# The last stores issued with their evictions, the last product in halves, and the prologue's work shared out anew

## The chip, the cores and the metric

The kernel runs on one NeuronCore of one Trainium2 chip. The metric is the device time of one execution in microseconds (us); what is compared is the median of several runs. The engines are called by the profile's names: PE is TensorE (matmul), DVE is VectorE, ACT is ScalarE, POOL is GpSimd, SP is SyncE, which issues nearly all DMAs here.

## The reference

Attention inside chunks of 64 tokens, then a feed-forward layer with softplus in its middle:

```python
def _attn_ref(q, k, v):                      # each 8 x 8 x 576 x 64 (batch, head, token, head_dim)
    q_c = q.reshape(B, H, nc, chunk, D)      # chunk = 64, so nc = 9; k_c and v_c alike
    scores = scale * np.matmul(q_c, k_c.transpose(0, 1, 2, 4, 3))
    scores = scores - np.max(scores, axis=-1, keepdims=True)
    attn = np.exp(scores)
    attn = attn / (np.sum(attn, axis=-1, keepdims=True) + 1e-09)
    return np.matmul(attn, v_c).reshape(B, H, S, D)

def _moe_ref(x, w_in, w_out):                # x 4608 x 512, w_in 512 x 2048, w_out 2048 x 512
    h = x @ w_in
    g = np.maximum(h, 0.0) + np.log1p(np.exp(-np.abs(h)))
    return g @ w_out
```

## The kernel before

**Tiling.** The 4608 tokens are 36 attention blocks of 128 tokens (two chunks, all eight heads), and nine row groups `m` of 512 tokens (four blocks, `TPM = 4` tiles each) for the two matrix products. The hidden width of 2048 is cut into 16 slices `fc` of 128. So there are 144 GEMM blocks `g = 16 m + fc`. Each has a first product `G1` (`gemm1`, L587: 12 matmuls of 128x512 into a PSUM tile `pa`), a softplus on ACT (`sp_g`, L595), a split of its result into a rounded part `g_hi` (`sp_hi`, L599, ACT) and a remainder `g_lo` (`sp_lo`, L603, DVE or POOL), and a second product `G2` (`gemm2`, L618: three terms for each of four tiles, added up in the PSUM tiles `po0` to `po3` over the 16 blocks of a row group). PE runs `G2` of a block behind `G1` of the next. In row group 0 both products run their three terms one after the other, `wi_lo` in the second term of `G1`, `x` low part in the third, `g_lo` in the third term of `G2`, so that late operands have more time.

**Split weights.** Each product is three f32r matmuls (high times high, high times low, low times high). The weights arrive as f32 in 32 units (`units`, numbered by when they are due; one for each `fc` of `w_in` and of `w_out`). Each unit is loaded (`w_load`, 512 KB) and decoded in five steps: `w_top` (L252, ACT or POOL), `w_low` (L261, ACT), `w_add` (L266, DVE, 128x1024), `w_hi` (L287, ACT or POOL) and `w_lo` (L291, DVE or POOL). `TOP_ACT`, `HI_POOL` and `LO_POOL` list the unit numbers that go to the engine in the list's name; `NORM_POOL` and `GLO_POOL` do the same for the division by the softmax sum (`att_norm`, L537, by attention block) and for `sp_lo` (by GEMM block).

**Attention.** The first four blocks (`FIRST_BLK = 4`) run on PE before the first GEMM block: transposes (`pe_t`), scores (`pe_s`), the subtraction of the row maximum as a matmul with a negated identity (`pe_sub`, L518, for blocks in `SUB_PE`; otherwise `att_sub`, L512, on DVE), exp on ACT, sum and reciprocal on DVE (`att_den`, L530), `att_norm`, a transpose (`pe_e`) and the product with V (`pe_v`, L403), whose result goes to `x` as a rounded part on ACT (`att_xh`, L562) and a remainder on DVE (`att_xl`, L566). All other blocks are transposed by DVE or DMA and run their PE work in pairs, as bursts (`blk_s` L462, `blk_v` L550) behind `G1` of GEMM blocks 4, 8, 15 and later ones. Their transposes on DVE are four small instructions (`blk_t4` L449 for `q` and `k`, `blk_e4` L486 for the weights after exp, for blocks in `SWAP_DVE`) or one (`blk_t` L439, `blk_e` L474).

**The order.** A list scheduler (`Plan`) simulates the engines with a written-in cost for each task, takes at each moment the ready task with the smallest `urg`, and emits the code in that order. The order so found is fixed: each engine runs its instructions in it and waits where an operand is late. `T0` and `TG` say when GEMM block `g` is due (`T0 + TG * g`), and the weights' and the bursts' urgencies follow from that; `VQ`, `KS`, `LQ` and `QK_URG` move other urgencies, `LOAD_AFTER`, `QK_AFTER` and `V_AFTER` name the load behind which the weight loads, the burst blocks' loads of `q` and `k`, and their loads of `v` may start.

**Filler matmuls.** Where the planner's own times leave PE a gap of more than 0.6 us before its time 90, `keep_warm` (L335) puts matmuls of the identity (`ident`) ahead of the task, whether or not the gap is there on the chip:

```python
    def keep_warm(dst):
        for _ in range(int(FILL * (plan.gap - 0.6) / 0.23)):     # FILL = 0.8
            nc.tensor.matmul(dst[:, :P], ident, ident, start=True, stop=True)
```

Such a matmul is f32 and stands in the trace as two records, in the order as one row.

**Halves.** With `HALVES = 2` GEMM blocks 0 and 1 each run as two pieces of two tiles (256 columns of `G1`), so that the first piece needs the attention of two blocks only.

**The end.** For the last row group, `evacuate` (L627) copies `po0` and `po2` on ACT and `po1` on DVE into `raw` tiles, tasks of their own (`store`, L632) send each 256 KB out over SP, and the fourth tile goes out as two halves (`last_half`: half a is copied and sent by ACT, half b copied by DVE and sent by SP, behind half a's copy).

Of the kernel before, what the change touches and what calls it, by code (L numbers as in the profile page):

```python
# [148 lines left out]
def chunked_attention_softplus_ffn(  # L149
# [9 lines left out]
    nc = tc.nc  # L159
    B, H, S, D = q.shape  # L160
    DM, DF = w_in.shape
    P = 128
# [444 lines left out]
    def gemm2(w):  # L607
        if w["first"]:
            pos.setdefault(w["m"], []).extend(po_tile(t) for t in w["tiles"])
        g_hi, g_lo, fc = w["hi"], w["lo"], w["fc"]  # L610
        w_hi_, w_lo_ = wo[fc]
        if w["first"]:
            keep_warm(pos[w["m"]][w["tiles"][0]])
        terms = ((g_hi, w_hi_), (g_hi, w_lo_), (g_lo, w_hi_))
        tiles = list(enumerate(w["tiles"]))
        order = [(n, j) for n in range(3) for j in tiles] if w["m"] < 1 else [(n, j) for j in tiles for n in range(3)]
        for n, (j, t) in order:
            nc.tensor.matmul(  # L618
                pos[w["m"]][t], terms[n][0][:, j * P : (j + 1) * P], terms[n][1],
                start=(w["first"] and n == 0), stop=(w["last"] and n == 2),  # L620
            )

    def evacuate(w, t):
        if t % 2 == 0:
            live["out", w["m"], t // 2] = raw_tile()
        o = live["out", w["m"], t // 2][:, t % 2 * DM : (t % 2 + 1) * DM].bitcast(F32)
        (nc.vector.tensor_copy if t % 2 else nc.scalar.copy)(o, pos[w["m"]][t])  # L627
        live["o", w["m"], t] = o

    def store(m, t):  # L630
        r0 = m * MT + t * P
        nc.sync.dma_start(out[r0 : r0 + P, :], live.pop(("o", m, t)))  # L632

    def last_half(w, j):
        m, t = w["m"], TPM - 1
# [4 lines left out]


    plan = Plan(raw=RAW_BUFS, top=TOP_BUFS, low=LOW_BUFS, po0=1, po1=1, po2=1, po3=1, pa=2, g=LAG + 1, u=1)
    HALVES = 2
    SPLIT = 0
    SUB_PE = (0, 1, 2, 3)
    SP_FREE = 1
    OFF = 0
    NOFF = 3
    T0, TG = 30.0, 5.2
    TK = (0,1)  # L650
    KS = 0.2
    VQ = -40
    LQ = -61
    HI_POOL = (1,3,5,6,7,8,9,10,12,13,15,17,19,20,21,25,27,28,30,31)
    WHOLE = (4,5,9)
    SWAP_DVE = (4,7,9)
    LOAD_POOL = ()
    TOP_ACT = (0,1,3,4,5,6,7,8,9,10,15,16,17,18,19,20,23,24,25,27,29,30)
    LOAD_AFTER = "v3"
    LO_POOL = (1,2,4,5,7,8,9,14,15,16,19,22,23,25,26,27,28,29,31)  # L660
    NORM_POOL = (0,2,3,4,5,6,7)
    GLO_POOL = (0,2,4,5,6,8,9,10,12,15,16,17,19)
    WO_AFTER = 1.1
    BEGIN = (4, 8, 15)
    BURST_AT = (6, 14)
    QK_AFTER = "v3"
    V_AFTER = "load10"
    K6_AFTER = "load13"
    QK_URG = 0
    T_URG = 0  # L670
    V_URG = 20
    SW_URG = 0
# [170 lines left out]
    for w in ahead + blocks:  # L843
# [21 lines left out]
        if w["last"]:  # L865
            for t in range(TPM):
                odd = t % 2
                if m == NM - 1 and t == TPM - 1:
                    for j in range(2):
                        plan.add(f"ev{m}_{t}" + "ab"[j], "DVE" if j else "ACT", 0.4, partial(last_half, w, j), [f"G2_{g}"],  # L870
                                 urg=-3, after=[f"ev{m}_{t - 1}"])
                    continue
                plan.add(f"ev{m}_{t}", "DVE" if odd else "ACT", 0.65, partial(evacuate, w, t), [f"G2_{g}"], urg=-3,
                         take=[] if odd else [("raw", [f"st{m}_{j}" for j in (t, t + 1) if m < NM - 1 or j < TPM - 1])],
                         after=[f"ev{m}_{t - 1}"] if odd else [])
                plan.add(f"st{m}_{t}", "SP", 0.6, partial(store, m, t), [f"ev{m}_{t}"], urg=1e5, kb=256)

    plan.emit()

# [33 lines left out]
```

## Time and profile before

| what | value |
|---|---|
| median of 3 runs | 862.52 us (862.5 to 862.55) |
| the profiled execution | 862.54 us |
| its span in the profile | 860.7 us (so 1.84 us lie around the span) |
| PE busy in the span | 848.0 us (99%) |
| DVE, ACT, POOL busy | 344.5, 313.7, 75.1 us (40%, 36%, 9%) |
| bytes moved | 63.13 MB, mean 73 GB/s |
| TensorE clock granted | 0.999 of full speed |

A busy engine need not be working at its peak, and idle time of the other engines costs nothing as such. Start times below are from the start of the span; a row that stands for several instructions gives their time together.

### The profile page before, as it was taken

To read this page: it belongs to the slowest core of one execution; us is meant where nothing else is said; L and a number is where in the kernel's file an instruction comes from. 1 tells how busy PE (TensorE), PEld (TensorE's weight loads), DVE (VectorE), ACT (ScalarE), POOL (GpSimd) and SP (SyncE) were. 2 spreads that over 40 slices of the span, in tenths; PEclk is the share of its full clock that TensorE was granted. 3 is DMA by queue.
4 is the path that set the end of the run, shared out by engine and by line. 5 is a ranking of instruction groups with operands and counts; after the bars stand their busy time and mean duration, and the time that the engine had idled before them with its cause. 6 is when DMAs were issued, how large, how long until landed. Compare 5 with 4: busy or idle time off the path is not lost.

```text
span 860.7 us, 14812 instructions
## 1 busy us (share of the span) xinstructions
PE 848.0 (99%) x5886; PEld 701.4 (81%) x5886; DVE 344.5 (40%) x600; ACT 313.7 (36%) x493; POOL 75.1 (9%) x76
## 2 busy tenths in 40 slices
PE   8899999999999999999999999999999999999997
PEld 7688888888888888888888888888888888888886
DVE  4989865333433241515252433324332514121111
ACT  3857744322423242424242423224232424232222
POOL 1576751000000000000000000000000000000000
PEclk9999999999999999999999999999999999999999
DMA  9887833222231224222322223222412241010001
GB/s 228 231 215 189 217 94 94 47 46 51 42 98 40 51 43 101 42 57 35 86 56 59 39 53 96 43 50 44 99 40 53 42 102 40 11 50 0 1 1 49
DMA packets 207061, 63.13 MB, mean 73 GB/s; under 512 B 184592, under 2 KB 200464, under 8 KB 206992
## 3 DMA queue, kind: packets, MB, share of 16 engines
q1 hardware_dynamic: 206848, 62.06, 31.6%
q8 instruction: 46, 0.75, 0.4%
q14 instruction: 23, 0.19, 0.1%
q10 hardware_dynamic: 144, 0.13, 0.0%
HBM read 45.09 MB, written 9.44 MB: 63 GB/s over the span
## 4 chain that ended last, share of the span: by engine, by line
PE 91%; DVE 3%; SPq 1%; DMA 1%; ACT 1%; issue 1%; POOL 0%; DVEq 0%; POOLq 0%; ACTq 0%
PE po L618 44%; PE pa L587 43%; PE pa L550 2%; PE pa L462 2%; SPq L318 1%; DMA raw<-in_moe_w_in_dram 1%; DMA raw<-in_moe_w_out_dram 1%; DVE qe L449 1%; DVE eT L486 0%; DVE ka L449 0%; ACT u L595 0%; DVE den L530 0%; DVE low L266 0%; DVE wib L266 0%; DVE x L566 0%
## 5 line engine op out<-in xcount | busy, mean ns | idle before, releaser
L595 ACT ACTIVATE u<-pa 128x512 f32<-128x512 f32 (+1 forms) x146 | 86.5, 593 | 505.5 <-PE pa L587 504.4
L603 DVE TENSOR_TENSOR g_lo<-u,g_hi 128x512 fp32r<-128x512 f32 (+1 forms) x133 | 92.5, 696 | 440.9 <-ACT g_hi L599 440.8
L587 PE MATMUL pa<-x,wib 128*128 128x512 f32 x864 | 207.6, 389 | 0.0
L587 PEld LDWEIGHTS pa<-x,wib 128*128 128x128 f32 x864 | 162.3, 188 | 33.6
L587 PE MATMUL pa<-x,wi_hi 128*128 128x512 f32 (+1 forms) x592 | 186.2, 384 | 0.0
L618 PE MATMUL po<-late,g_hi 128*128 128x512 f32 x540 | 166.8, 392 | 0.1
L587 PEld LDWEIGHTS pa<-x,wi_hi 128*128 128x128 f32 x592 | 109.7, 188 | 22.0
L618 PEld LDWEIGHTS po<-late,g_hi 128*128 128x128 f32 x540 | 100.7, 188 | 21.7 <-POOL late L291 0.5
L618 PE MATMUL po<-wo_hi,g_hi 128*128 128x512 f32 x288 | 109.7, 393 | 0.0
L618 PE MATMUL po<-wo_lo,g_hi 128*128 128x512 f32 x288 | 108.9, 390 | 0.6 <-POOL wo_lo L291 0.6
L618 PE MATMUL po<-wo_hi,g_lo 128*128 128x512 f32 x288 | 108.8, 390 | 0.0
L587 PE MATMUL pa<-x,wi_lo 128*128 128x512 f32 (+1 forms) x296 | 108.7, 384 | 0.0
L618 PE MATMUL po<-late,g_lo 128*128 128x512 f32 x288 | 108.3, 390 | 0.0
L599 ACT CAST g_hi<-u 128x512 fp32r<-128x512 f32 (+1 forms) x146 | 89.8, 615 | 4.4
L618 PEld LDWEIGHTS po<-wo_lo,g_hi 128*128 128x128 f32 x288 | 54.0, 188 | 12.0 <-POOL wo_lo L291 1.0
L587 PEld LDWEIGHTS pa<-x,wi_lo 128*128 128x128 f32 x296 | 54.8, 188 | 10.9
L618 PEld LDWEIGHTS po<-wo_hi,g_lo 128*128 128x128 f32 x288 | 54.0, 188 | 11.6 <-DVE g_lo L603 0.3
L618 PEld LDWEIGHTS po<-late,g_lo 128*128 128x128 f32 x288 | 54.1, 188 | 11.3
L618 PEld LDWEIGHTS po<-wo_hi,g_hi 128*128 128x128 f32 x288 | 53.7, 188 | 11.3
L530 DVE TENSOR_REDUCE den<-qe 128x8 f32<-128x512 f32 x32 | 21.2, 662 | 24.9 <-ACT qe L525 24.9
L566 DVE TENSOR_TENSOR x<-pa,x 128x512 fp32r<-128x512 f32 x36 | 24.5, 683 | 1.9 <-ACT x L562 1.8
L439 DVE STREAM_TRANSPOSE ka<-k 128x512 f32<-128x512 f32 x28 | 19.8, 706 | 13.4 <-DMA eT<-ka 13.4
(108 smaller groups left out, 578.2 us busy)
## 6 DMA issues: line engine op xcount, KB each, us to landing
out_dram<-raw SPq DMA_DIRECT2D x35, 256.0 KB, 2.4
raw<-in_moe_w_in_dram SPq DMA_DIRECT2D x16, 512.0 KB, 5.0
raw<-in_moe_w_out_dram SPq DMA_DIRECT2D x16, 512.0 KB, 4.4
eT<-ka SPq DMA_DIRECT2D x232, 32.0 KB, 1.9
q<-in_q_dram SPq DMA_DIRECT2D x224, 32.0 KB, 2.2
k<-in_k_dram SPq DMA_DIRECT2D x224, 32.0 KB, 2.1
q<-in_v_dram SPq DMA_DIRECT2D x60, 64.0 KB, 2.4
k<-in_v_dram SPq DMA_DIRECT2D x60, 64.0 KB, 2.4
```

The source lines that it names most:

```text
L318: eng.dma_start(dst[p0 : p0 + rows], src[b, :, s0 : s0 + rows, :].rearrange("h s d -> s h d"))
L439: nc.vector.transpose(t, live.pop((n, i)))
L449: nc.vector.transpose(dst[d : d + BL, :, tb], src[s : s + BL, :, dh])
L462: nc.tensor.matmul(pa[o, c2, col : col + C], qT[r, a * HP + hl, :], kT[r, a * HP + hl, :], start=True, stop=True,)
L530: nc.vector.tensor_reduce(den, e, axis=AX.X, op=ALU.add)
L550: nc.tensor.matmul(pa[o, a, col : col + C], vt[r, 4 * j + 2 * h2 + c2, :], eT[r, :, 4 * c2 + 2 * j + h2, :], start=True, stop=True,)
L566: nc.vector.tensor_tensor(lo, live.pop(("xp", i)), hi.bitcast(F32), op=ALU.subtract)
L587: nc.tensor.matmul(ph, wt[:, c, fs], x[:, ts_, c, :], start=(n == 0), stop=(n == 3 * KC - 1))
L595: nc.scalar.activation(w["u"], w["ph"], AF.Softplus)
L599: nc.scalar.copy(w["hi"], w["u"])
L603: (nc.gpsimd if pool else nc.vector).tensor_tensor(w["lo"], w["u"], w["hi"].bitcast(F32), op=ALU.subtract)
L618: nc.tensor.matmul(pos[w["m"]][t], terms[n][0][:, j * P : (j + 1) * P], terms[n][1], start=(w["first"] and n == 0), stop=(w["last"] and n ...
```

## The change

The last row group's stores are no longer tasks of the plan: `evacuate` issues each right behind its copy. The last tile's `G2` of the last block leaves `gemm2` and becomes two tasks, `GZ0` and `GZ1` (`last_product`: three matmuls of 256 columns each), and each half's eviction waits for its own task. `HALVES` becomes 0, so blocks 0 and 1 run whole. Block 1 leaves `SUB_PE`, so its subtraction runs on DVE. The remaining edits are new values of the planner's parameters: which units and blocks go to which engine, and when things are due.

```diff
--- before.py
+++ after.py
@@ -615,9 +615,12 @@
         tiles = list(enumerate(w["tiles"]))
         order = [(n, j) for n in range(3) for j in tiles] if w["m"] < 1 else [(n, j) for j in tiles for n in range(3)]
         for n, (j, t) in order:
+            if w["g"] == NG - 1 and t == TPM - 1:
+                w["end"] = terms
+                continue
             nc.tensor.matmul(
                 pos[w["m"]][t], terms[n][0][:, j * P : (j + 1) * P], terms[n][1],
-                start=(w["first"] and n == 0), stop=(w["last"] and n == 2),
+                start=(w["first"] and n == 0), stop=n == 2 and (w["last"] or w["g"] == NG - 2 and t == TPM - 1),
             )
 
     def evacuate(w, t):
@@ -626,10 +629,20 @@
         o = live["out", w["m"], t // 2][:, t % 2 * DM : (t % 2 + 1) * DM].bitcast(F32)
         (nc.vector.tensor_copy if t % 2 else nc.scalar.copy)(o, pos[w["m"]][t])
         live["o", w["m"], t] = o
+        if w["m"] == NM - 1:
+            store(w["m"], t)
 
     def store(m, t):
         r0 = m * MT + t * P
         nc.sync.dma_start(out[r0 : r0 + P, :], live.pop(("o", m, t)))
+
+    def last_product(w, j):
+        cols = slice(j * DM // 2, (j + 1) * DM // 2)
+        for n, (g, wt) in enumerate(w["end"]):
+            nc.tensor.matmul(
+                pos[w["m"]][TPM - 1][:, cols], g[:, (TPM - 1) * P :], wt[:, cols], start=False, stop=n == 2,
+                skip_group_check=True,
+            )
 
     def last_half(w, j):
         m, t = w["m"], TPM - 1
@@ -640,33 +653,33 @@
 
 
     plan = Plan(raw=RAW_BUFS, top=TOP_BUFS, low=LOW_BUFS, po0=1, po1=1, po2=1, po3=1, pa=2, g=LAG + 1, u=1)
-    HALVES = 2
+    HALVES = 0
     SPLIT = 0
-    SUB_PE = (0, 1, 2, 3)
+    SUB_PE = (0,2,3)
     SP_FREE = 1
     OFF = 0
-    NOFF = 3
-    T0, TG = 30.0, 5.2
-    TK = (0,1)
-    KS = 0.2
-    VQ = -40
+    NOFF = 1
+    T0, TG = 28.0, 5.5
+    TK = (0,2)
+    KS = 0.4
+    VQ = -55
     LQ = -61
-    HI_POOL = (1,3,5,6,7,8,9,10,12,13,15,17,19,20,21,25,27,28,30,31)
+    HI_POOL = (1,2,3,4,5,6,7,8,10,12,15,17,19,20,21,25,30,31)
     WHOLE = (4,5,9)
-    SWAP_DVE = (4,7,9)
+    SWAP_DVE = (4,7,8,9)
     LOAD_POOL = ()
-    TOP_ACT = (0,1,3,4,5,6,7,8,9,10,15,16,17,18,19,20,23,24,25,27,29,30)
-    LOAD_AFTER = "v3"
-    LO_POOL = (1,2,4,5,7,8,9,14,15,16,19,22,23,25,26,27,28,29,31)
-    NORM_POOL = (0,2,3,4,5,6,7)
-    GLO_POOL = (0,2,4,5,6,8,9,10,12,15,16,17,19)
+    TOP_ACT = (0,3,4,5,6,7,8,9,10,14,15,18,19,20,23,24,25,27,29,30)
+    LOAD_AFTER = "v2"
+    LO_POOL = (0,1,2,3,4,5,7,8,9,14,15,16,19,22,25,26,27,29,30,31)
+    NORM_POOL = (0,1,3,5,6,7)
+    GLO_POOL = (2,4,5,6,8,9,10,11,12,16,19)
     WO_AFTER = 1.1
     BEGIN = (4, 8, 15)
     BURST_AT = (6, 14)
-    QK_AFTER = "v3"
-    V_AFTER = "load10"
+    QK_AFTER = "load2"
+    V_AFTER = "load8"
     K6_AFTER = "load13"
-    QK_URG = 0
+    QK_URG = 10
     T_URG = 0
     V_URG = 20
     SW_URG = 0
@@ -867,13 +880,15 @@
                 odd = t % 2
                 if m == NM - 1 and t == TPM - 1:
                     for j in range(2):
-                        plan.add(f"ev{m}_{t}" + "ab"[j], "DVE" if j else "ACT", 0.4, partial(last_half, w, j), [f"G2_{g}"],
+                        plan.add(f"GZ{j}", "PE", 0.36, partial(last_product, w, j), [f"GZ{j - 1}" if j else f"G2_{g}"], urg=1e6)
+                        plan.add(f"ev{m}_{t}" + "ab"[j], "DVE" if j else "ACT", 0.4, partial(last_half, w, j), [f"GZ{j}"],
                                  urg=-3, after=[f"ev{m}_{t - 1}"])
                     continue
                 plan.add(f"ev{m}_{t}", "DVE" if odd else "ACT", 0.65, partial(evacuate, w, t), [f"G2_{g}"], urg=-3,
-                         take=[] if odd else [("raw", [f"st{m}_{j}" for j in (t, t + 1) if m < NM - 1 or j < TPM - 1])],
+                         take=[] if odd else [("raw", [f"st{m}_{j}" for j in (t, t + 1)] if m < NM - 1 else [])],
                          after=[f"ev{m}_{t - 1}"] if odd else [])
-                plan.add(f"st{m}_{t}", "SP", 0.6, partial(store, m, t), [f"ev{m}_{t}"], urg=1e5, kb=256)
+                if m < NM - 1:
+                    plan.add(f"st{m}_{t}", "SP", 0.6, partial(store, m, t), [f"ev{m}_{t}"], urg=1e5, kb=256)
 
     plan.emit()
 
```

What the new values do is seen in the order of instructions on each engine. Three places follow.

The first is DVE around the first `g_lo` (L603). Before, that instruction follows one group of four small transposes (L449), and it covers half a block:

```order
L566 TENSOR_TENSOR x<-pa,x 128x512
L449 STREAM_TRANSPOSE qe<-q 32x8x32 x4
L566 TENSOR_TENSOR x<-pa,x 128x512
L266 ISA wib<-wib,top_102 128x1024
L449 STREAM_TRANSPOSE ka<-k 32x8x32 x4
L603 TENSOR_TENSOR g_lo<-u,g_hi 128x256
L266 ISA wib<-wib,top_101 128x1024
L291 TENSOR_TENSOR wi_lo<-wib,wi_hi 128x4x128
L449 STREAM_TRANSPOSE ka<-k 32x8x32 x4
```

Now, with the whole block:

```order
L566 TENSOR_TENSOR x<-pa,x 128x512
L266 ISA wib<-wib,top_102 128x1024
L566 TENSOR_TENSOR x<-pa,x 128x512
L266 ISA wib<-wib,top_101 128x1024
L449 STREAM_TRANSPOSE qe<-q 32x8x32 x4
L266 ISA wib<-wib,top_102 128x1024
L449 STREAM_TRANSPOSE ka<-k 32x8x32 x4
L449 STREAM_TRANSPOSE qe<-x 32x8x32 x4
L603 TENSOR_TENSOR g_lo<-u,g_hi 128x512
L266 ISA wib<-wib,top_101 128x1024
L266 ISA wib<-wib,top_102 128x1024
```

The four transposes that stood between the last two of the four `x` remainders (L566) have moved behind them; ahead of the first `g_lo` there now stand two adds (L266) and three groups of transposes, where there was one of each behind the last L566. The `wi_lo` between the first two `g_lo` is gone (POOL has it now).

The second place is DVE and PE ahead of GEMM block 7, the last that needs a `wi_lo` written by DVE in this stretch (its second term). On DVE, before:

```order
L266 ISA wib<-wib,top_102 128x1024
L266 ISA wib<-wib,top_101 128x1024
L291 TENSOR_TENSOR wi_lo<-wib,wi_hi 128x4x128
L530 TENSOR_REDUCE den<-qe 128x8
L531 TENSOR_SCALAR den<-den 128x8
L532 RECIPROCAL den<-den 128x8
L530 TENSOR_REDUCE den<-qe 128x8
L531 TENSOR_SCALAR den<-den 128x8
L532 RECIPROCAL den<-den 128x8
L266 ISA low<-low,top_102 128x1024
L486 STREAM_TRANSPOSE eT<-qe 32x256 x4
L474 STREAM_TRANSPOSE ka<-qe 128x512
```

Now:

```order
L530 TENSOR_REDUCE den<-qe 128x8
L531 TENSOR_SCALAR den<-den 128x8
L532 RECIPROCAL den<-den 128x8
L530 TENSOR_REDUCE den<-qe 128x8
L531 TENSOR_SCALAR den<-den 128x8
L532 RECIPROCAL den<-den 128x8
L537 TENSOR_TENSOR qe<-qe,den 128x512
L266 ISA wib<-wib,top_101 128x1024
L486 STREAM_TRANSPOSE eT<-qe 32x256 x4
L474 STREAM_TRANSPOSE ka<-qe 128x512
L486 STREAM_TRANSPOSE eT<-qe 32x256 x4
L291 TENSOR_TENSOR wi_lo<-wib,wi_hi 128x4x128
```

The `wi_lo` row (L291) stood ahead of the sums of blocks 4 and 5 (L530 to L532). It now stands last, behind those, the division of block 4 (L537, now on DVE), an add, and nine transposes (eight small L486, one L474). On PE the end of block 5's `G2` and block 7's `G1` (L587), before:

```order
L618 MATMUL po_499<-wo_hi,g_lo 128x512
L618 MATMUL po_500<-wo_hi,g_lo 128x512
L618 MATMUL po_582<-wo_hi,g_lo 128x512
L618 MATMUL po_583<-wo_hi,g_lo 128x512
L587 MATMUL pa<-x,wi_hi 128x512 x4
L587 MATMUL pa<-x,wi_lo 128x512 x4
```

Now:

```order
L621 MATMUL po_504<-wo_hi,g_lo 128x512
L621 MATMUL po_505<-wo_hi,g_lo 128x512
L621 MATMUL po_506<-wo_hi,g_lo 128x512
L621 MATMUL po_507<-wo_hi,g_lo 128x512
L335 MATMUL pa<-ident 128x128 x11
L587 MATMUL pa<-x,wi_hi 128x512 x4
```

Eleven filler matmuls (L335) now stand between them.

The third place is SP's end: the stores (two `raw` tiles, the first with output tiles 0 and 1, the second with 2 and 3). Before:

```order
L632 DMA out_0_dram<-raw_7397 128x512 x2
L632 DMA out_0_dram<-raw_7399 128x512 x2
L632 DMA out_0_dram<-raw_7875 128x512
L639 DMA out_0_dram<-raw_7877 128x256
L632 DMA out_0_dram<-raw_7875 128x512
L632 DMA out_0_dram<-raw_7877 128x512
```

Now:

```order
L637 DMA out_0_dram<-raw_7366 128x512 x2
L637 DMA out_0_dram<-raw_7368 128x512 x2
L637 DMA out_0_dram<-raw_7844 128x512
L637 DMA out_0_dram<-raw_7850 128x512
L637 DMA out_0_dram<-raw_7844 128x512
L652 DMA out_0_dram<-raw_7850 128x256
```

The half tile (128x256) stood second of the last four and now stands last; tile 2's store comes ahead of tile 1's.

## Rows read from the trace of the kernel before

**Rows 1.** Busy us by stretch: five engines, then clock, DMA share, GB/s.
```profile
20.00:30.00 10.00, 6.97 (x125) 4.85 (x124) 9.33 (x20) 8.70 (x17) 4.76 (x5) 1.00 1.11 240
...
140.00:850.00 710.00, 709.94 (x4723) 587.88 (x4722) 231.84 (x399) 222.04 (x343) 1.28 (x1) 1.00 0.24 50
```

**Rows 2.** Timeline of PE: start, length, line, what, [idle before it <- who ended it].
```profile
8.11 0.39 PE L335 MATMUL po<-ident 128*128 128x128 f32 x2
...
24.51 0.61 PE L335 MATMUL po<-ident 128*128 128x128 f32 x4
...
29.45 0.71 PE L335 MATMUL pa<-ident 128*128 128x128 f32 x4 [1.06 <-DVE x L566]
...
31.99 0.49 PE L335 MATMUL pa<-ident 128*128 128x128 f32 x2 [0.40 <-DVE x L566]
...
37.96 0.74 PE L618 MATMUL po<-wo_lo,g_hi 128*128 128x512 f32 x2 [0.61 <-POOL wo_lo L291]
...
39.01 0.64 PE L587 MATMUL pa<-x,wi_hi 128*128 128x256 f32 x4
...
41.83 1.07 PE L587 MATMUL pa<-x,wi_hi 128*128 128x512 f32 x4
...
54.16 1.45 PE L462 MATMUL pa<-ka,qe 64*64 64x64 f32 x64
...
63.84 1.07 PE L587 MATMUL pa<-x,wi_hi 128*128 128x512 f32 x4
...
69.28 1.07 PE L587 MATMUL pa<-x,wi_hi 128*128 128x512 f32 x4
```

**Rows 3.** Timelines of DVE between 24 and 52 us, and of POOL at 41.
```profile
24.14 1.03 DVE L291 TENSOR_TENSOR wi_lo<-wib,wi_hi 128x512 fp32r<-128x512 f32 x1
...
29.42 1.79 DVE L449 STREAM_TRANSPOSE qe<-q 32x256 f32<-32x256 f32 x4
31.25 0.69 DVE L566 TENSOR_TENSOR x<-pa,x 128x512 fp32r<-128x512 f32 x1
...
32.45 1.77 DVE L449 STREAM_TRANSPOSE ka<-k 32x256 f32<-32x256 f32 x4
34.25 0.42 DVE L603 TENSOR_TENSOR g_lo<-u,g_hi 128x256 fp32r<-128x256 f32 x1
...
41.12 2.41 DVE L266 CUSTOM_DVE_ANT_0 wib<-wib,top 128x1024 uint16<-128x1024 uint16 x2
...
49.69 1.80 DVE L449 STREAM_TRANSPOSE ka<-x 32x256 f32<-32x256 f32 x4
...
41.09 1.29 POOL L291 TENSOR_TENSOR wi_lo<-wib,wi_hi 128x512 fp32r<-128x512 f32 x1
```

**Rows 4.** Timeline of DVE between 62 and 73 us.
```profile
62.23 0.69 DVE L291 TENSOR_TENSOR wi_lo<-wib,wi_hi 128x512 fp32r<-128x512 f32 x1 [0.51 <-POOL wi_hi L287]
64.61 0.69 DVE L530 TENSOR_REDUCE den<-qe 128x8 f32<-128x512 f32 x1 [1.69 <-ACT qe L525]
...
67.17 1.37 DVE L266 CUSTOM_DVE_ANT_0 low<-low,top 128x1024 uint16<-128x1024 uint16 x1
68.46 1.77 DVE L486 STREAM_TRANSPOSE eT<-qe 32x256 f32<-32x256 f32 x4
70.26 0.71 DVE L474 STREAM_TRANSPOSE ka<-qe 128x512 f32<-128x512 f32 x1
```

**Rows 5.** Timeline of PE at the burst behind block 8.
```profile
80.14 0.69 PE L462 MATMUL pa<-ka,qe 64*64 64x64 f32 x32 [0.64 <-DVE ka L439]
```

**Rows 6.** The end: SP's and ACT's timeline, then the stores' times to landing.
```profile
856.24 0.33 SPq L639 DMA_DIRECT2D out_dram<-raw  x1
856.62 0.96 SPq L632 DMA_DIRECT2D out_dram<-raw  x2
...
854.70 0.59 ACT L627 COPY raw<-po 128x512 f32<-128x512 f32 x1 [0.77 <-PE po L618]
...
DMA to landing us min/median/max: 2.0/2.2/2.3
```

## The prediction

> **What bounds the kernel now.** First the busy time by stretch: from 140 to 850 us PE is busy for 709.94 of 710 us at full clock [rows 1]. There only added or removed matmuls could move time, and this change keeps them as they are. So time can move at two ends: in the prologue, where PE is busy 6.97 of 10 us between 20 and 30 [rows 1] and waits, and behind the last matmul. Second the timeline of PE, for the prologue's waits: 1.06 us at 29.45 and 0.40 at 31.99 for the `x` remainders of DVE, 0.61 at 37.96 for a `wo_lo` of POOL [rows 2], then 0.64 at 80.14 for a transpose of DVE [rows 5]. Third the timeline of DVE, which is what PE mostly waits for: in 20 to 30 it is busy 9.33 of 10 us [rows 1]. Two measures for later: a GEMM block costs PE 69.28 - 63.84 = 5.44 us, so 0.227 a matmul [rows 2]; a filler costs 0.61 - 0.39 = 0.22 (two take 0.61, one 0.39) [rows 2].
>
> The sum is made against the profiled execution, 862.54 us (span 860.7 and 1.84 around it), which is the median, 862.52, but for 0.02.
>
> **Part 1, the lead at block 6.** Call L how much earlier than at 63.84 [rows 2] PE reaches the `G1` of block 6.
>
> *Start of block 0.* Before, the first half starts behind two fillers at 29.45 + 0.44 = 29.9. The fourth `x` remainder ends at 31.25 + 0.69 = 31.94 [rows 3]. In the new order three things that stood ahead of it are gone: four transposes (1.79), a `wi_lo` (1.03) [rows 3], and one add, at most half of the 2.41 for two [rows 3]. That puts it at 27.9 to 29.1; I take 28.5. A whole `G1` needs it in its third term, 1.8 us (8 x 0.227) after its start, so it may start at 26.7. PE's own attention work ended at 29.45 - 1.06 = 28.4 before [rows 2] and now loses one subtraction to DVE; I take 27.5, between the two. Gain 2.4 (1.5 to 3.2). The weight loads start one load earlier on SP, which I count in this range and not beside it.
>
> *Waits that go.* 0.40 and a filler of 0.22 at 31.99 (between the two half pieces), 0.61 at 37.96 (that `wo_lo` is now wanted by a whole block, later): gain 1.2. Whole blocks instead of halves: four 256-column matmuls take 0.64, four of 512 take 1.07 [rows 2], so two pieces cost at most 0.21 more for each group of four; the records overlap, so the true size lies between 0 and 6 x 0.21; I take 0.2.
>
> *A wait that comes.* `G2` of block 0 wants `g_lo` in its third term: 27.5 + 2 x 2.72 + a filler 0.2 + 1.8 = 34.9. DVE now runs, behind the fourth remainder (28.5), two adds, three groups of four transposes and then the `g_lo`: 28.5 + 2 x 0.7 + 3 x 1.8 + 0.7 = 36.0 (transposes by the 1.77 at 32.45; add and whole-block `g_lo` by 0.7, the price of the 128x512 operations in [rows 3] and [rows 4], since the half-block `g_lo` of 0.42 is too small). Before, one group stood there and the `g_lo` came at 34.25 [rows 3]. An add that meets a POOL instruction takes longer: two take 2.41 at 41.12, where POOL works from 41.09 to 42.38 [rows 3], about 1.0 more than 1.4. So the wait is 1.1 to 2.1; I take 1.5, between the ends, as one of two adds meeting POOL is as likely as not. What waits behind it on DVE are the next adds, hence the decoding.
>
> *The burst behind block 4* (54.16 before [rows 2]). It wants the last `ka`, which DVE ended at 49.69 + 1.80 = 51.49 [rows 3], 16.8 us after the first `g_lo`. The new order has one group of transposes (1.8) and one `w_lo` (0.7 to 1.0) less there, but two whole `g_lo` for two halves (0.6 more): 14.8, so `ka` ends at 50.8 to 51.9. PE wants it around 52.5. It is just in time; each add that meets POOL (1.0) goes to PE. I take 0.4 (0 to 1.5).
>
> L = 2.4 + 1.2 + 0.2 - 0.2 (filler ahead of the first `G2`) - 1.5 - 0.4 = 1.7 us (0.4 to 3.2).
>
> **Part 2, block 7 gives it back.** Eleven fillers stand ahead of its `G1`, wanted or not: 11 x 0.22 = 2.4 us. And `wi_lo` for its second term, which before was done at 62.23 + 0.69 = 62.9 [rows 4], before the softmax sums, now comes behind them. The sums start when exp is done, at 64.61 [rows 4]; exp follows block 5's softplus on ACT, so it moves with PE, to 64.61 - L. From there: two sums, 67.17 - 64.61 = 2.6 (of which I let 0.4 be one slow piece), the division 0.7, an add 0.7 (1.37 where it meets POOL), transposes 1.8 + 0.7 + 1.8, `wi_lo` 0.7 [rows 4]: 8.6 to 9.6. So it is done at 73.2 - L to 74.2 - L, and `G1`, which needs it 0.9 after its start, can run without a stop from 72.3 - L to 73.3 - L, where before it ran at 69.28. Block 7 costs 3.0 to 4.0 us; the fillers lie inside this, so it is no less than 2.4. I take 3.3: PE is then 1.6 later than before.
>
> Here a page speaks too. The pair of adds at 41.12 ran long just where POOL had begun a subtraction at 41.09 [rows 3]. The Trainium skill (SBUF — State Buffer, "Who interferes with whom") says that a VectorE instruction with two SBUF inputs and a GpSimd instruction that reads SBUF exclude each other, the first to issue holding the port for its whole length. This trace agrees with that, and by it the change, which hands more `w_lo` and `w_hi` to POOL in this stretch, risks more such meetings; in the sum it would turn 3.3 into 4.0.
>
> **Part 3, the burst behind block 8.** The 0.64 at 80.14 [rows 5] may go, PE being later than DVE there, or DVE's longer queue ahead of that burst (one add more) and its later `g_lo` may hold the PSUM tile for block 9: -0.6 to +0.9, I take +0.2. What the lists move behind that costs nothing: from 140 us on DVE is busy 232 of 710 us [rows 1], with POOL empty, which is the cover; if it failed it would show as a wait of a few tenths.
>
> **Part 4, the end.** Before, two whole stores wait on SP behind the half tile: it goes at 856.24, they at 856.62 (0.96 for both) though tile 2's copy ended at 854.70 + 0.59 = 855.29. A whole store lands 2.0 to 2.3 after its issue [rows 6], so the last of the two, issued at about 857.1, lands at 859.4. Now tile 2 goes at 855.3, tile 1 at about 855.8, the half at about 856.3. Tile 1 then lands at 855.8 + 2.2 = 858.0, and the half, which is no slower than a whole store, by 856.3 + 2.3 = 858.6, perhaps 0.1 more behind the others: the last landing comes at 858.0 to 858.7. Gain 0.7 to 1.4, I take 1.0. The last product's halves (6 matmuls for 3 whole ones, 0 to 0.1 us) free half a's copy a little earlier; ACT's copy of tile 2 ends at 855.29 anyway. I cost them at nothing. [...]
>
> **Sum:** -1.7 + 3.3 + 0.2 - 1.0 = +0.8; 862.54 + 0.8 = 863.3 us.
>
> **The rivals.** About 0.2% (1.7 us) is what a measurement of this kernel can tell from no change.
> - *Forecast: the lead is spent at block 7, the end pays back part.* L of 0.9 to 2.9 with the middle values elsewhere, 862.1 to 864.1, and up to the bound: chance 0.46.
> - *Slower: adds meet POOL.* Both the `g_lo` wait (2.1) and the burst's (1.0) take their dear side, so L is 0.5, and block 7 costs 4.0: -0.5 + 4.0 + 0.2 - 1.0 = +2.7, 865.2. It decides from two meetings on. For it: DVE is nearly full, and 41.12 and 67.17 show such meetings [rows 3, 4]; against it: DVE has given a `wi_lo` to POOL. Chance 0.27.
> - *Faster: the lead is larger and the cheap side holds.* L of 3.0 (`x` remainders early, no stop at the burst), block 7 at 3.0, the wait at 80.14 gone, the end 1.3: -3.0 + 3.0 - 0.6 - 1.3 = -1.9, 860.6. For it: DVE loses work that PE waited for; against it: eleven fillers run in any case. Chance 0.25.
> - *The clock.* If PE's new wait at block 7 let TensorE fall from 2.4 to 1.2 GHz, one block would take about 5.4 us more: 868.7. The clock stood at full between 20 and 30 us with PE busy only 6.97 of 10 [rows 1], and fillers precede that wait. Chance 0.02. The Trainium skill (TensorE: Matmul & The Clock Gate, "HAM oscillation") warns of idle gaps between bursts; no row of this prologue shows a fall.
> - *The end gives nothing*, as the transfers' last landing is set by something else: 864.3, within the first case's bound.
>
> Range: from the faster case's 860.6 to the slower one's 865.2, which leaves out about 2 in 10; the likeliest alone is 862.1 to 864.2. Faster by over 0.2%: 0.25; within: 0.46; slower: 0.29.
>
> **What would show it.** Part 1: first whole `G1` at about 27.5; a wait of 1 to 2 us in the third term of the first `G2` on a `g_lo` of DVE. Part 2: 22 filler records ahead of block 7's `G1`, and then a stop in it or ahead of it on a `wi_lo` (L291) of DVE; block 7 later than 69.28. Part 4: stores in the order tile 0, 2, 1, half, the last landing 0.7 to 1.4 us nearer to the last matmul. It is wrong if block 7 starts earlier than 69.28, or if waits over 0.5 us come behind 130 us.

## The result and the profile after

The changed kernel takes 863.97 us (median of 14 runs, 863.74 to 865.2), the kernel before beside it 862.33 (14 runs, 861.59 to 865.53): a ratio of 1.0019 with a 95% interval of 1.0012 to 1.0025, so +1.64 us. The forecast was 863.3, with 860.6 to 865.2 around it.

The profiled execution of the change was the longest of its 14 (865.2 us, span 863.3), and it holds an event of its own, read first. The windows of the changed kernel (columns as in [rows 1]):

```profile
26.00:32.00 6.00, 4.93 (x41) 3.59 (x41) 5.17 (x9) 3.05 (x6) 3.82 (x5) 0.50 0.89 219
...
140.00:850.00 710.00, 709.94 (x4724) 587.91 (x4723) 238.90 (x415) 223.12 (x344) 1.29 (x1) 1.00 0.23 50
```

And its timeline of PE there:

```profile
24.95 0.66 PE L387 MATMUL po<-ident,x 128*128 128x128 f32 x4 [1.35 <-POOL x L537]
...
29.34 2.07 PE L587 MATMUL pa<-x,wi_hi 128*128 128x512 f32 x4
```

From 26 to 32 us the granted clock is 0.50 (1.2 GHz), after an idle of 1.35 us at 24.95; four matmuls of the first `G1` take 2.07 us where they take 1.07 in [rows 2]. From 140 to 850 us PE is busy for 709.94 us, as before [rows 1]: the change lies in the two ends alone. The same program run and profiled again (experiment 1) keeps a clock of 1.00 there and takes 864.26 us. Its timeline of PE is the one to hold against [rows 2] and [rows 5]:

```profile
27.55 1.19 PE L587 MATMUL pa<-x,wi_hi 128*128 128x512 f32 x4
...
34.13 1.17 PE L621 MATMUL po<-wo_hi,g_hi 128*128 128x512 f32 x4 [0.64 <-ACT g_hi L599]
...
37.02 1.20 PE L621 MATMUL po<-wo_hi,g_lo 128*128 128x512 f32 x4 [0.80 <-DVE g_lo L603]
...
61.86 1.07 PE L587 MATMUL pa<-x,wi_hi 128*128 128x512 f32 x4
...
67.30 2.62 PE L335 MATMUL pa<-ident 128*128 128x128 f32 x22
69.67 1.18 PE L587 MATMUL pa<-x,wi_hi 128*128 128x512 f32 x4
71.80 1.19 PE L587 MATMUL pa<-x,wi_lo 128*128 128x512 f32 x4 [0.95 <-DVE wi_lo L291]
...
76.48 2.88 PE L587 MATMUL pa<-x,wib 128*128 128x512 f32 x12
...
85.73 2.99 PE L587 MATMUL pa<-x,wib 128*128 128x512 f32 x12 [1.14 <-POOL wib L291]
...
118.65 3.23 PE L587 MATMUL pa<-x,wib 128*128 128x512 f32 x12
121.81 0.70 PE L550 MATMUL pa<-eT,q 64*64 64x64 f32 x32
...
123.47 0.51 PE L550 MATMUL pa<-eT,k 64*64 64x64 f32 x19 [0.26 <-DMA k<-in_v_dram]
...
127.34 0.39 PE L587 MATMUL pa<-x,wi_hi 128*128 128x512 f32 x1
```

The same places in the timeline of the kernel before, as far as [rows 2] do not have them:

```profile
74.72 2.88 PE L587 MATMUL pa<-x,wib 128*128 128x512 f32 x12
...
83.62 2.88 PE L587 MATMUL pa<-x,wib 128*128 128x512 f32 x12
...
116.72 2.89 PE L587 MATMUL pa<-x,wib 128*128 128x512 f32 x12
119.54 0.69 PE L550 MATMUL pa<-eT,q 64*64 64x64 f32 x32
...
124.42 0.39 PE L587 MATMUL pa<-x,wi_hi 128*128 128x512 f32 x1
...
854.96 0.39 PE L618 MATMUL po<-late,g_lo 128*128 128x512 f32 x1
```

Read as distances: the change is 63.84 - 61.86 = 1.98 us ahead at block 6, 1.76 behind at block 8 (76.48), 2.11 behind at block 9 (85.73), and 127.34 - 124.42 = 2.92 behind at block 16, from where PE runs without a stop.

The end of that execution, timelines of SP and PE, against [rows 6]:

```profile
856.87 2.17 SPq L637 DMA_DIRECT2D out_dram<-raw  x3
859.18 0.36 SPq L652 DMA_DIRECT2D out_dram<-raw  x1
...
858.01 0.28 PE L642 MATMUL po<-late,g_lo 128*128 128x256 f32 x1
```

The half now goes last, at 859.18, and the whole stores ahead of it. The span ends at 862.5, 4.21 us behind the last matmul (858.01 + 0.28); before it was 860.7 - 855.35 = 5.35 (its last matmul ends at 854.96 + 0.39). So the end gives 1.14, and 2.92 - 1.14 = +1.78 us is what the two spans differ by (862.5 and 860.7).

### The profile page after: what moved, and what is told of

Its sections match the earlier page's. It is cut to its first block, busy times and chain, and to the rows that moved or that the text cites. A ratio compares the mean times of both kernels' runs of the same rounds, so it can differ in the third digit from the quotient of the medians.

```text
span 863.3 us, 14792 instructions
## 1 busy us (share of the span) xinstructions
PE 851.1 (99%) x5879; PEld 703.1 (81%) x5879; DVE 350.4 (41%) x608; ACT 313.6 (36%) x489; POOL 74.1 (9%) x74
## 4 chain that ended last, share of the span: by engine, by line
PE 90%; DVE 3%; SPq 2%; DMA 2%; ACT 1%; issue 1%; POOL 1%; DVEq 0%; POOLq 0%; ACTq 0%
PE pa L587 43%; PE po L621 43%; PE pa L550 2%; PE pa L462 1%; DMA raw<-in_moe_w_out_dram 1%; SPq L318 1%; DVE ka L449 1%; DVE wib L266 1%; SPq L239 0%; DVE g_lo L603 0%; SPq L432 0%; DMA k<-in_v_dram 0%; DMA x<-in_k_dram 0%; ACT top L252 0%; SPq L327 0%
## 5 line engine op out<-in xcount | busy, mean ns | idle before, releaser
L603 DVE TENSOR_TENSOR g_lo<-u,g_hi 128x512 fp32r<-128x512 f32 x133 | 94.3, 709 | 445.3 <-ACT g_hi L599 445.1
L595 ACT ACTIVATE u<-pa 128x512 f32<-128x512 f32 x144 | 86.1, 598 | 501.1 <-PE pa L587 500.0
L587 PE MATMUL pa<-x,wib 128*128 128x512 f32 x864 | 208.0, 389 | 1.2 <-POOL wib L291 1.1
L587 PEld LDWEIGHTS pa<-x,wib 128*128 128x128 f32 x864 | 162.0, 188 | 35.7 <-POOL wib L291 2.0
L587 PE MATMUL pa<-x,wi_hi 128*128 128x512 f32 x576 | 186.1, 391 | 0.0
L587 PEld LDWEIGHTS pa<-x,wi_hi 128*128 128x128 f32 x576 | 108.5, 189 | 22.8 <-ACT x L562 0.2
L587 PE MATMUL pa<-x,wi_lo 128*128 128x512 f32 x288 | 108.9, 392 | 0.9 <-DVE wi_lo L291 0.9
L599 ACT CAST g_hi<-u 128x512 fp32r<-128x512 f32 x144 | 89.4, 621 | 4.3
L587 PEld LDWEIGHTS pa<-x,wi_lo 128*128 128x128 f32 x288 | 54.6, 190 | 12.8 <-DVE wi_lo L291 1.4
L530 DVE TENSOR_REDUCE den<-qe 128x8 f32<-128x512 f32 x32 | 21.2, 661 | 24.7 <-ACT qe L525 24.7
L566 DVE TENSOR_TENSOR x<-pa,x 128x512 fp32r<-128x512 f32 x36 | 24.5, 682 | 1.1 <-ACT x L562 1.1
```

Of the source, the lines that this page charges most:

```text
L530: nc.vector.tensor_reduce(den, e, axis=AX.X, op=ALU.add)
L566: nc.vector.tensor_tensor(lo, live.pop(("xp", i)), hi.bitcast(F32), op=ALU.subtract)
L587: nc.tensor.matmul(ph, wt[:, c, fs], x[:, ts_, c, :], start=(n == 0), stop=(n == 3 * KC - 1))
L595: nc.scalar.activation(w["u"], w["ph"], AF.Softplus)
L599: nc.scalar.copy(w["hi"], w["u"])
L603: (nc.gpsimd if pool else nc.vector).tensor_tensor(w["lo"], w["u"], w["hi"].bitcast(F32), op=ALU.subtract)
```

## The experiments

Each ratio is to runs of the kernel before taken beside it, with its 95% interval. Edits are shown against the changed kernel, those of experiments 9 and 10 against experiment 4; `...` marks lines left out. Experiments 3, 5, 8, 11 and 12 insert four lines, so that their line numbers are 4 larger.

**1. The changed kernel again,** with no edit.

> The changed kernel once more, unaltered. In its profile TensorE's clock was granted at half from about 25.5 to 32.5 us, and the time of that execution, 865.2, lies 1.2 above the median of its runs. Theory: the fall belongs to that execution and a few more; then the time here is 863.7 to 864.1, the granted clock over the run 0.999 to 1.000, and most of the 1.6 us by which the change is slower has other causes. Rival: the clock falls in each execution and costs over 1 us; then the granted clock is again 0.995 to 0.997.

Measured: 864.07 us, 1.0016 [1.0007, 1.0025]. The half clock at 26 to 32 us does not come back, and block 6 starts at 61.86 where the first profile has it at 62.99, 1.1 later: that is the price of the event in one execution, and no part of the median (12 of the 14 runs of the result have a granted clock of 0.998 to 1.000).

**2. Without the eleven fillers ahead of block 7.**

```diff
-                self.gap = start - last if start < self.WARM_UNTIL else 0.0
+                self.gap = start - last if start < self.WARM_UNTIL and t["name"] not in ('G1_7',) else 0.0
```

> The changed kernel without the eleven fillers ahead of block 7. Theory of the prediction (the late wi_lo sets block 7, the fillers lie inside that wait): within 0.3 us of the changed kernel, and the profile shows a wait of about 3.3 us on wi_lo in the second term of block 7's first product, which then starts 2.4 us earlier. Rival, the fillers are the cost: 2.4 us faster than the changed kernel. Rival, the clock: the wait without fillers lets TensorE's clock fall, 1 to 2 us slower.

Measured: 865.64 us, 1.0037 [1.0025, 1.005], 1.6 slower than with them. Its timeline of PE in block 7 and at the start of block 8:

```profile
71.76 1.87 PE L587 MATMUL pa<-x,wi_lo 128*128 128x512 f32 x4 [3.43 <-DVE wi_lo L291]
...
78.04 2.88 PE L587 MATMUL pa<-x,wib 128*128 128x512 f32 x12
```

And one of its windows:

```profile
72.00:74.00 2.00, 2.00 (x6) 1.54 (x6) 2.00 (x4) 0.62 (x1) 1.62 (x2) 0.51 0.91 335
```

The second term starts at 71.76 without fillers and at 71.80 with them: the `wi_lo` sets it and not the fillers. But behind the 3.43 us of idle time the clock is 0.51 (0.64 in the two microseconds after these), and block 8 starts 1.56 later (78.04). The fillers cost nothing here and hold the clock at 2.4 GHz.

**3. The `wi_lo` of block 7 early, and no fillers.** The unit's `w_hi` (on POOL now) and `w_lo` go ahead of attention block 4's exp and sums.

```diff
+        for name, other in (('w_hi13', 'exp4'), ('w_lo13', 'den4')):
+            task = next(x for x in todo if x[1]["name"] == name)
+            todo.remove(task)
+            todo.insert(next(n for n, x in enumerate(todo) if x[1]["name"] == other), task)
...
+                self.gap = start - last if start < self.WARM_UNTIL and t["name"] not in ('G1_7',) else 0.0
...
+    HI_POOL += (13,)
```

> The changed kernel without the fillers, with the w_hi of the unit of block 7 on POOL and its wi_lo on DVE ahead of the softmax sums, where the kernel before had it. Theory 1 (block 7 alone spends the lead): block 7 starts at about 68.4 or earlier, and the time is 3.0 us below the changed kernel's, about 861. Theory 2 (DVE's queue up to the burst behind block 8 is late as a whole, so the next operands become the wait): block 8 and that burst take most of it back, and the time is 1 to 1.5 us below the changed kernel's, about 862.7.

Measured: 861.84 us, 2.2 below experiment 1, between what the theories gave; the ratio is 1.0002 [0.9993, 1.0011], since 3 of its 11 runs lie at 864.1 to 865.2, which the median doesn't show. Its timeline of PE:

```profile
67.12 1.07 PE L591 MATMUL pa<-x,wi_hi 128*128 128x512 f32 x4
...
72.90 1.20 PE L591 MATMUL pa<-x,wib 128*128 128x512 f32 x4 [0.17 <-POOL wib L291]
74.84 2.11 PE L591 MATMUL pa<-x,wib 128*128 128x512 f32 x8 [0.74 <-POOL wib L295]
...
78.59 0.69 PE L554 MATMUL pa<-eT,x 64*64 64x64 f32 x30 [0.26 <-DMA eT<-ka]
79.71 0.69 PE L466 MATMUL pa<-ka,qe 64*64 64x64 f32 x32 [0.43 <-DVE ka L443]
...
83.40 2.99 PE L591 MATMUL pa<-x,wib 128*128 128x512 f32 x12
```

The wait at block 7 is gone, and block 7 starts 2.16 us earlier than before (69.28). By block 9 the waits shown (0.17, 0.74, 0.26, 0.43; the kernel before has only the 0.64 of [rows 5] there) have left 0.22 of it (83.62 before). So it is block 7's late `wi_lo` that held PE there, and with it early the fillers must go too (experiment 5); but the lead then meets operands that no engine has ready earlier.

**4. The new end alone,** with the parameters of before.

```diff
-    HALVES = 0
+    HALVES = 2
...
-    T0, TG = 28.0, 5.5
+    T0, TG = 30.0, 5.2
...
-    QK_AFTER = "load2"
-    V_AFTER = "load8"
+    QK_AFTER = "v3"
+    V_AFTER = "load10"
```

> The kernel before with the end of the changed one alone: stores issued with the evictions, last product in halves, all planner parameters as before. Theory of the prediction: 0.7 to 1.4 us faster than before, 1.0 in the middle (861.3), with the stores of tiles 2 and 1 issued ahead of the half tile. Rival, the end gives nothing because something else sets the last landing: within 0.2 of before.

Measured: 861.37 us, 0.9991 [0.9982, 1.0]; by the medians the end gives 1.25.

**5. The `wi_lo` early, fillers kept:** the move of experiment 3, without the edit on `self.gap`.

```diff
+        for name, other in (('w_hi13', 'exp4'), ('w_lo13', 'den4')):
...
+    HI_POOL += (13,)
```

> As e3 (w_hi of block 7's unit on POOL, its wi_lo ahead of the softmax sums), but with the eleven fillers kept. Theory 1 (behind block 7 other late operands set the time, as e3's waits of 0.17 and 0.74 us for POOL at block 8 and 0.26 and 0.43 at the burst behind it say): the 2.4 us of fillers are paid mostly out of those waits, and the time is within 0.6 us of e3's 861.84. Theory 2 (with the operand early each filler counts): 2.4 us above e3, about 864.2, as the changed kernel.

Measured: 862.75 us, 1.0005 [0.9996, 1.0014], 0.9 above experiment 3. Block 7 starts behind the fillers at 69.43 without a wait, block 8 at 75.00 and block 9 at 84.25, 0.85 behind experiment 3. Where no operand is late, 2.4 us of fillers are a cost, of which the waits behind them take back 1.5.

**6. The new parameters alone,** with the end of before.

```diff
-        if w["m"] == NM - 1:
-            store(w["m"], t)
...
-                        plan.add(f"GZ{j}", "PE", 0.36, partial(last_product, w, j), [f"GZ{j - 1}" if j else f"G2_{g}"], urg=1e6)
...
```

> The changed kernel's prologue (all planner parameters) with the end of the kernel before. Theory (the end and the prologue add up): above the changed kernel by what e4 gained, 1.2 us, so 865.2 to 865.4, which is 2.8 above the kernel before. Rival (the changed order also moves the end, or the end's gain needs it): within 0.4 of the changed kernel.

Measured: 864.93 us, 1.0026 [1.0016, 1.0037]. Its 2.40 above before and the 1.25 of experiment 4 make +1.15, and the whole change measured +1.45 in experiment 1 and +1.64 in the result: the end and the new parameters add up to within some tenths.

**7. Whole blocks alone:** the new end and `HALVES = 0`, all other parameters of before (`HALVES` stays out of the edit of experiment 4).

```diff
-    SUB_PE = (0,2,3)
+    SUB_PE = (0, 1, 2, 3)
...
-    T0, TG = 28.0, 5.5
+    T0, TG = 30.0, 5.2
...
```

> e4 (end alone) with HALVES = 0, all other parameters as before; the planner then finds an order of its own. Theory (the parts of the change need each other: whole blocks move the softmax weights of block 5 and ka later against PE, which is why the change also adds to the lists): PE is about 1 us earlier than before at blocks 5 to 8 and loses 2 to 4 us at the burst behind block 8, so 862.5 to 864.5, slower than e4. Rival (whole blocks are the gain of the prologue and the shared lists its loss): 0.5 to 1.5 us faster than e4's 861.37.

Measured: 866.66 us, 1.0045 [1.0032, 1.0058]: slower than experiment 4, as the theory had it, but 2.2 above the top of its range. Its timeline of PE:

```profile
27.52 0.66 PE L387 MATMUL po<-ident,late 128*128 128x128 f32 x4 [2.46 <-POOL late L537]
...
31.24 1.17 PE L587 MATMUL pa<-x,wi_hi 128*128 128x512 f32 x4
...
80.00 0.29 PE L550 MATMUL pa<-eT,x 64*64 64x64 f32 x2 [1.52 <-ACT low L261]
...
83.24 1.14 PE L462 MATMUL pa<-ka,qe 64*64 64x64 f32 x32 [1.22 <-DVE ka L439]
```

And one of its windows:

```profile
82.00:86.00 4.00, 2.78 (x38) 2.35 (x37) 3.83 (x7) 1.86 (x4) 2.65 (x3) 0.50 0.98 254
```

Block 0 starts at 31.24, 3.7 us later than in the change: whole blocks by themselves do not start early; in the change they do, with the work around them shared out anew. And with the waits at the burst of block 8 the clock falls to 0.50 there.

**8. The new end, and an earlier `ka` at the burst of block 8:** the parameters of before, and one transpose ahead of a weight's remainder.

```diff
+        for name, other in (('Tk7', 'w_lo17'),):
...
```

> e4 (end alone) with one move: the last ka transpose ahead of the burst behind block 8 (the wait of 0.64 us at 80.14 in the kernel before) is put on DVE ahead of the two weight remainders that stood before it. Theory: the wait goes, and DVE's subtraction that frees the PSUM tile for block 9 is the next in line, so 0.2 to 0.6 us less than e4, about 861.0. Rival (the remainders put behind are then late): 0 to 1 us more than e4.

Measured: 862.15 us, 0.9996 [0.9987, 1.0005], no better than experiment 4. The wait of [rows 5] falls from 0.64 to 0.26, and one of 1.27 us appears ahead of block 9: in the profiled execution (863.32 us, 1.2 above the median) the stall removed here is paid one block on.

**9. The stores alone:** as experiment 4, but the last product left whole.

```diff
-            if w["g"] == NG - 1 and t == TPM - 1:
-                w["end"] = terms
-                continue
...
```

> The kernel before with the stores of the last row group issued behind their evictions, the last product left whole. Theory (the order of the stores is the whole gain of the end, the halves give nothing, as the prediction cost them): as e4, 0.9 to 1.3 us below the kernel before. Rival (the halves matter, since half a is copied before the product ends): 0.3 us or more above e4.

**10. The last product's halves alone:** as experiment 4, but the stores left as tasks.

```diff
-        if w["m"] == NM - 1:
-            store(w["m"], t)
...
```

> The kernel before with the last product in halves and the stores as before. Theory (half a's copy on ACT follows tile 2's copy on the same engine, and the two whole stores still go behind the half tile on SP): within 0.3 us of the kernel before. Rival (half a free earlier lets half b and the stores behind it go earlier): 0.3 to 0.5 us below the kernel before.

Measured: experiment 9 at 861.52 us, 0.9985 [0.9976, 0.9993]; experiment 10 at 862.69, 0.9998 [0.9989, 1.0006]. SP's timeline with the stores alone:

```profile
853.55 2.16 SPq L634 DMA_DIRECT2D out_dram<-raw  x3
855.83 0.38 SPq L649 DMA_DIRECT2D out_dram<-raw  x1
```

With the halves alone the order is that of [rows 6]: the half at 855.86, the last two whole stores from 856.24. The order of the stores is the whole gain (1.07 us), though the half tiles take 2.4 to 2.6 us from issue to landing behind the whole ones (L649) and 1.7 ahead of them (L650). The halves of the product give nothing. Of all that ran, the end alone (experiments 4 and 9) is the version that beats both kernels; for experiment 9 the interval shows it.

**11. DVE's remainder of unit 18 behind a subtraction.** Ahead of block 9, DVE's `w_lo` goes behind attention block 6's `att_sub` in the changed kernel.

```diff
+        for name, other in (('w_lo18', 'max7'),):
...
```

> The changed kernel with one move: the remainder of wo unit 18 (L291 on DVE, which waits 1.4 us for ACT at 81.7) is put behind the first subtraction of the burst behind block 8. Theory (the 1.1 us wait of block 9's first product is for that subtraction, which frees the PSUM tile, though the profile names POOL's wib): the wait shrinks to about 0.5 us, and the time is 0.3 to 0.7 us below the changed kernel's 864.0. Rival (the releaser is POOL's remainder of a later unit, as the profile infers): the wait stays at 1.0 us or more, the time within 0.2.

Measured: 863.30 us, 1.0007 [0.9998, 1.0016], 0.8 below experiment 1. Timelines of PE, DVE (the subtraction) and POOL:

```profile
85.20 3.00 PE L591 MATMUL pa<-x,wib 128*128 128x512 f32 x12 [0.52 <-POOL wib L295]
...
84.36 0.69 DVE L516 TENSOR_TENSOR qe<-pa,mx 128x512 f32<-128x512 f32 x1
...
83.89 1.28 POOL L295 TENSOR_TENSOR wib<-low,wib 128x512 fp32r<-128x512 f32 x1
```

The subtraction in experiment 1, on DVE's timeline:

```profile
84.89 0.69 DVE L512 TENSOR_TENSOR qe<-pa,mx 128x512 f32<-128x512 f32 x1
```

The wait ahead of block 9 shrinks from 1.14 to 0.52. The subtraction, which reads a PSUM tile that `G1` of block 9 must write, ends 0.5 us earlier (at 85.05; 85.58 in experiment 1). The POOL instruction that the profile names ends 0.5 earlier too (85.17; 85.67), so that the times alone do not tell the two apart. The kernel does (`LO_POOL` has 19 and not 17): that POOL instruction writes the remainder of unit 19, which block 10 reads; block 9 reads unit 17, whose remainder DVE had done at 78.39 + 0.69 = 79.08 in experiment 1. So block 9 waits for the subtraction, as the theory had it, and starts 0.15 us behind its end in both runs (85.20; 85.73); the releaser that the profile infers is a bystander.

**12. Experiments 3 and 11 together.**

```diff
+        for name, other in (('w_hi13', 'exp4'), ('w_lo13', 'den4'), ('w_lo18', 'max7')):
...
```

> e3 (no fillers, block 7's wi_lo early) with the move of e11. Theory: e3's 861.84 less 0 to 0.4 us, since e3 hardly waits at block 9: about 861.6, within 0.3 of e4 (861.37), so that the changed prologue, mended, is no better than the old one. Rival (the lead of 2 us at block 6 now lasts): 860.5 or less.

Measured: 862.22 us, 0.9992 [0.9978, 1.0005]; 0.6 above what was expected and no better than experiment 3. Block 9 starts at 83.86 without a wait, but the burst ahead of it now waits 0.78 for a DMA of `eT`.

## Why the prediction was right, and where its terms were off

| step | predicted | measured (experiment 1) |
|---|---|---|
| lead at block 6 | -1.7 (-3.2 to -0.4) | -1.98 |
| block 7 | +3.3 (3.0 to 4.0) | +3.74 (1.98 + 1.76) |
| burst behind block 8 | +0.2 (-0.6 to +0.9) | +0.35 (2.11 - 1.76) |
| what the lists move behind that | 0 | +0.81 (2.92 - 2.11) |
| the end | -1.0 (-1.4 to -0.7) | -1.14 |
| sum | +0.8 | +1.78; by the medians +1.64 |

The way and the path came as forecast; the size is half of what was measured, and of the 1.0 that the sum lacks 0.81 is one term, on which Part 3 below.

**Part 1 held.** Block 0 starts at 27.55 (27.5 predicted) and DVE's fourth remainder ends at 28.44 (28.5). By the starts of rows the lead is 2.36 at block 0 (2.4 predicted), +0.05 between blocks 0 and 3 (which starts at 43.50, at 45.91 before; -0.3 predicted) and -0.43 at the burst behind block 4 (1.81 us instead of 1.38; -0.4 predicted). DVE's timeline at the first `g_lo`, and POOL's, in experiment 1:

```profile
27.75 0.69 DVE L566 TENSOR_TENSOR x<-pa,x 128x512 fp32r<-128x512 f32 x1
28.36 0.77 DVE L266 CUSTOM_DVE_ANT_0 wib<-wib,top 128x1024 uint16<-128x1024 uint16 x1
...
30.99 1.77 DVE L266 CUSTOM_DVE_ANT_0 wib<-wib,top 128x1024 uint16<-128x1024 uint16 x1
...
30.92 1.29 POOL L291 TENSOR_TENSOR wo_lo<-wib,wo_hi 128x512 fp32r<-128x512 f32 x1
```

One of the two adds behind that remainder met POOL at length, as the middle value had it: 1.77 us at 30.99 with POOL at work from 30.92, and 0.77 at 28.36. The Trainium skill (SBUF — State Buffer, "Who interferes with whom") has a VectorE instruction with two SBUF inputs and a GpSimd instruction that reads SBUF exclude each other, and this row agrees. The stop is 1.44 us (1.5 predicted), in two pieces: 0.80 for `g_lo`, under the 1 to 2 us that the prediction looked for, and 0.64 for ACT's `g_hi`, which it did not name. That the two make up the predicted size is luck.

**Part 2 held, at the dear end.** The fillers take 69.67 - 67.30 = 2.37 us (2.4). The `wi_lo` is done at 71.05 + 0.69 = 71.74, inside the 71.2 to 72.2 that a lead of 1.98 gives. The add in that queue met POOL (1.53 at 65.22 in DVE's timeline). What experiment 2 adds is that the fillers were no loss: the step's "no less than 2.4" was never the limit. The rival *adds meet POOL* got its meetings (1.77 at 30.99, 1.53 at 65.22) but not its price: the stop for `g_lo` was 0.80 and not 2.1, the burst's 0.43 and not 1.0. *The clock* was a rival with 0.02, priced at 5.4 us, and did not decide the median; but it stood behind the fillers, as experiment 2 shows (1.6 us), and the first profile of the change has it in the prologue.

**Part 3's second sentence was the mis-sized term.** "What the lists move behind that costs nothing" went by DVE's load behind 140 us. Between 100 and 120 us DVE was busy for 17.80 of 20 us in the kernel before, and the 0.81 comes at the end of that stretch, all of it in block 15 and its burst (block 15 starts 118.65 - 116.72 = 1.93 behind, block 16 2.92). Timelines of DVE, SP, POOL and PE's weight loads, in experiment 1:

```profile
115.92 0.69 DVE L291 TENSOR_TENSOR late<-low,late 128x512 fp32r<-128x512 f32 x1
116.53 0.68 DVE L266 CUSTOM_DVE_ANT_0 low<-low,top 128x1024 uint16<-128x1024 uint16 x1
117.25 1.79 DVE L449 STREAM_TRANSPOSE ka<-k 32x256 f32<-32x256 f32 x4
...
119.07 2.58 SPq L327 DMA_DIRECT2D k<-in_v_dram  x4
...
118.42 1.29 POOL L291 TENSOR_TENSOR wib<-low,wib 128x512 fp32r<-128x512 f32 x1 [5.37 <-ACT wib L287]
...
119.77 1.69 PEld L587 LDWEIGHTS pa<-x,wib 128*128 128x128 f32 x8 [0.47 <-POOL wib L291]
```

The same in the kernel before:

```profile
111.56 1.28 DVE L266 CUSTOM_DVE_ANT_0 low<-low,top 128x1024 uint16<-128x1024 uint16 x2
112.88 1.80 DVE L449 STREAM_TRANSPOSE ka<-k 32x256 f32<-32x256 f32 x4
...
114.70 2.58 SPq L327 DMA_DIRECT2D k<-in_v_dram  x4
...
114.64 1.29 POOL L291 TENSOR_TENSOR wib<-low,wib 128x512 fp32r<-128x512 f32 x1
```

DVE's queue is 4.4 us behind there. An earlier group of transposes of `k` has moved behind a `g_lo` that waits for ACT (to 114.12, from 109.15), and a remainder that the new `LO_POOL` takes from POOL stands ahead of the add (115.92). Two operands of PE hang on that queue. SP's load of `v` for the burst takes the buffer that the last transposes of `k` free (SP waited 4.5 us for them by the view of waits): it goes out right behind them, at 119.07 where it went at 114.70, 4.4 us later while PE is 1.9 later; PE then waits for that DMA at 123.47. And the remainder that block 15's `G1` reads second is done 3.8 us later on POOL: its `w_hi` is on ACT in both kernels, but comes behind DVE's add, done at 117.21 instead of 112.84. The first costs about 0.6 (121.81 to 124.44 against 119.54 to 121.57), the second about 0.3 (118.65 to 121.81 against 116.72 to 119.54). This is read from the rows; a kernel with those instructions moved back was not tried. In experiments 3, 5, 11 and 12 the wait for `v` stands as well (0.19 to 0.36). The wait that Part 3's first sentence allowed for came where it was put, ahead of block 9, for the subtraction that frees the PSUM tile (experiment 11), while the one of [rows 5] went.

**Part 4 held as a sum** (1.14 in the profile, 1.25 and 1.07 in experiments 4 and 9). Its premise that the half is "no slower than a whole store" (2.3) did not: 2.4 to 2.6. It cost little, as the half left SP 0.1 earlier than reckoned (855.77 in experiment 4, with the last matmul done at 854.88).

## What to carry to other kernels

A lead won at the start is worth what the next late operand leaves of it: before a prologue is reordered, follow each moved list entry to the buffer it frees and the load that waits for that buffer, out to where the matmuls run without a stop. Filler matmuls are to be priced with the wait they stand in: here they cost nothing and kept the clock where the operand behind them was late, and were a loss where it was ready. At the end, issue the large stores as soon as their copies are done and let the small one go last, even if it lands slower there.

## What the hardware showed unexpectedly

TensorE's clock fell from 2.4 to 1.2 GHz after an idle time of 1.35 us (24.95 in the first profile of the change), but not after 2.46 us in experiment 7 (27.52; granted clock 1.00 from 24 to 36 us); experiment 2 has a fall after 3.43 us and experiment 7 one at the waits of 1.52 and 1.22. So the length of one idle time did not tell here whether the clock falls. The Trainium skill (TensorE: Matmul & The Clock Gate, "HAM oscillation — how this bites in real kernels") warns of idle gaps between bursts of matmuls; these runs agree that such gaps can bring it about, at a cost of 1.1 and 1.6 us in the two cases that could be read (experiments 1 and 2). A 128 KB store took 1.7 us to land when it went ahead of two of 256 KB and 2.4 to 2.6 when it went behind them.
